# A second layer whose first product is formed from seven block products, with a one-pass softplus

## The chip, the cores and the metric

The kernel runs on one core of a Trainium2 chip. The core has a matrix engine (PE, with its weight loads shown apart as PEld), a vector engine (DVE), an activation engine (ACT), a general engine (POOL), and a queue engine (SP) that issues the transfers here. The metric is the device time of one execution in microseconds, as the median of several runs.

## The reference

Three layers follow one another. All inputs are float32 on the host side apart from the weights, which arrive as 64-bit floats.

```python
x = attention(q, k, v)                  # linear attention, 4 batches x 576 tokens, 8 heads of 64
x = x / rms(x) * rms_g                  # 2304 tokens x 512
x = (silu(x @ w_gate) * (x @ w_val)) @ w_out        # 512 -> 1536 -> 512
h = x @ w2_in                           # 512 -> 2048
g = np.maximum(h, 0) + np.log1p(np.exp(-np.abs(h)))  # softplus
out = g @ w2_out                        # 2048 -> 512
```

## The kernel before

Tokens are cut into NB = 6 blocks of T = 384. Each operand of the two feed-forward layers is split in a high and a low float32r half, and each product is three matrix products (`mm3`, lines 538 to 541: high by high, high by low, low by high). A column tile of a hidden layer is 128 columns wide: 12 tiles in the first layer (FA), 16 in the second (FB). The model dimension of 512 is four row tiles (KD).

The program order of every engine is written out by hand. The string ORDER lists the attention and the first 15 steps of the first layer, mixed. `busy` (B in the list) adds matrix products that compute nothing. From line 775 a loop runs the other 57 of the 72 steps of the first layer (stage A here). A step is one column tile of one token block: `g` (12 matrix products), `v` (12), then the output product `o_step` of the step before (12). After `v`, DVE multiplies (`a`, line 793), ACT rounds to the high half (line 795), and DVE subtracts to get the low half (line 797). Column tiles are taken in groups (GA = 3, 4, 5); the token blocks run inside a group. So one block has 3, 4 or 5 steps in a row. After the last of them the four sums in PSUM are added to `x2t` by DVE (`x2_out`, line 589), and the four input tiles of the next block are split again (`halves`, lines 528 and 536).

The second layer (stage B, from line 857) has 96 steps. One step is `h` for one column tile of one block (12 matrix products of 384 columns), softplus in four ACT and three DVE passes (lines 867 to 882), and the output product `y_step` of two steps earlier (9 matrix products of 512 columns). Sums over a group of column tiles (GB = 6, 5, 5) are added to an SBUF tile by `y_out`. The input tiles of the next block are split by ACT and POOL on the way.

Weights are fetched as 64-bit numbers (`fetch`) and turned into the two halves on the chip: `convert_a` (ACT), `convert_l` and three `convert_d` (DVE), `convert_c` (ACT), `convert_s` (DVE in stage A, POOL in stage B). `at_place(i, p, ...)` puts such a piece at place p of step i, and `do(i, p)` issues it there. Each of the 32 weight tiles of layer two is converted once for the kernel and used by all six blocks of its group.

Of the kernel before, what the change touches and what calls it, by code (L numbers as in the profile page):

```python
# [25 lines left out]
LQ.0.0 LK.0.1.1 Q0.0.0 LX.0 MX.0 LK.0.2.2 QS.0.0.1.P LK.0.0.1 QS.0.0.0.P K0.0.1.1.V QE.0.0.1 QE.0.0.0 K0.0.2.2.V  # L26
LQ.0.1 MV F.7 QR.0.0 B.22 K1.0.2 K0.0.0.1.V LQ.0.2 QI.0.0 KM.0.2 B.2 K1.0.0 CA.7 KM.0.0 F.6 QM.0.0.1.P QM.0.0.0.P
LQ.1.0 K2.0.0 Q0.0.1 KS.0.0 LG Q0.0.2 QS.0.1.1.P LK.1.0.2 QS.0.1.0.P K2.0.2 CL.7.V QE.0.1.0 QS.0.2.0.V T.1 CA.6 KS.0.2
QE.0.2.0 QE.0.1.1 KE.0.0 CL.6.V Q0.1.0 LV.0.0.4 TC.1.A MK LX.1 CD.7.0 QS.1.0.1.P QR.0.1 QI.0.1 QS.1.0.0.P F.3 QE.1.0.1
MX.1 QR.0.2.0 QE.1.0.0 T.0 CA.3 LW.0 LV.0.4.8 QR.1.0 K0.1.0.2.V CD.7.1 KE.0.2 B.28 K3.0.0 CL.3.V CD.7.2 QM.0.1.0.P  # L30
QI.0.2.0 CD.6.0 T.2 QM.0.1.1.P QI.1.0 CD.6.1 K1.1.0 LQ.1.1 TC.0.A QM.1.0.0.P KM.1.0 F.0 TC.2.A QM.0.2.0.P K3.0.2
K4.0.0 K2.1.0 Q0.1.1 LK.1.2.2 K4.0.2 KS.1.0 X0.0.0 X0.0.1 LV.1.0.4 CA.0 SQ.0.1 XG.0.1.A LW.1 XG.0.0.A QS.1.1.1.P
CL.0.V X0.0.2 KE.1.0 K0.1.2.2.V B.4 K1.1.2 X0.0.3 CD.3.0 CD.6.2 XG.0.2.A SQ.0.0 QS.1.1.0.P KM.1.2 F.2 CD.3.1
XS.0.0.1.V K2.1.2 LV.1.4.8 SQ.0.2 QE.1.1.0 QE.1.1.1 SQ.0.3 T.5 XS.0.2.3.P TC.5.A T.3 KS.1.2 F.1 K3.1.0 LX.2 CD.0.0
XS.0.0.2.P CA.2 T.4 QR.1.1 K4.1.0 CL.2.V CD.3.2 CD.0.1 LK.2.0.2 QI.1.1 KE.1.2 CC.7 CA.1 XG.0.3.A TC.4.A QM.1.0.1.P
MX.2 K3.1.2 CL.1.V X1.0 LQ.2.0 TC.3.A B.1 X0.1.1 K4.1.2 CD.1.0 X0.1.3 XG.1.3.A CD.0.2 LK.2.2.2 K0.2.0.2.V X0.1.0
SQ.1.1 XD.0 XG.1.1.A QM.1.1.1.P CD.1.1 Q0.2.0 X0.1.2 SQ.1.2 CC.0 XP.0 LW.2 XG.1.2.A LV.2.0.4 QM.1.1.0.P K1.2.0 CC.3
KM.2.0 SQ.1.3 QS.2.0.0.P T.8 B.1 K2.2.0 T.7 TC.8.A SQ.1.0 TC.7.A T.6 X2.0 K0.2.2.2.V TC.6.A K1.2.2 KS.2.0 KM.2.2
X0.2.0 X0.2.1 XS.1.2.3.V K2.2.2 LV.2.4.8 X3.0.1 F.4 XG.1.0.A CC.6 X3.0.0 X3.0.2 KE.2.0 HH.0.0.A QS.2.0.1.P XS.1.0.1.P
CS.0.P HH.0.2.A HH.0.1.A HL.0.0.P KS.2.2 F.5 HL.0.1.P XS.1.0.2.V K3.2.0 X3.0.3 LQ.2.1 CA.4 LK.3.0.2 G.0.0 LV.3.0.4  # L40
CD.2.0 CL.4.V X1.1 CD.1.2 KE.2.2 HH.0.3.A CC.1 SQ.2.0 LK.3.2.2 CA.5 HL.0.2.V CD.4.0 CD.2.1 HL.0.3.V G.0.1 CS.3.V
CS.1.V K3.2.2 G.0.2 QE.2.0.0 CL.5.V G.0.3 CD.4.1 QE.2.0.1 XD.1 CD.4.2 XP.1 K4.2.2 CD.5.0 MX.3 S.0 V.0 Q0.2.1 CD.5.1
G.1.0 X0.2.2 CC.4 G.1.1 A.0 CS.7.P X2.1 CS.4.P X3.1.2 G.1.2 CS.6.P G.1.3 CD.5.2 S.1 V.1 F.8 X3.1.1 X3.1.0 CC.5 SQ.2.2
QR.2.0 CD.2.2 G.2.0 CS.5.P X3.1.3 G.2.1 QI.2.0 CC.2 G.2.2 HH.1.0.A AH.0.A QM.2.0.1.V XG.2.2.A XG.2.0.A X0.2.3 XG.2.1.A
QS.2.1.0.P G.2.3 A.1 QM.2.0.0.P HL.1.0.V SQ.2.1 T.10 K4.2.0 SQ.2.3 S.2 V.2 LX.3 AL.0.V CS.2.P HH.1.3.A HH.1.1.A G.3.0
F.15 XS.2.0.1.V XG.2.3.A TC.10.A HL.1.3.V HH.1.2.A XS.2.2.3.P XS.2.0.2.V AH.1.A HL.1.1.V CA.8 O.0 HL.1.2.V G.3.1 X1.2
QE.2.1.0 AL.1.P QS.2.1.1.P G.3.2 QE.2.1.1 CL.8.V CA.15 A.2 T.9 TC.9.A CD.8.0 CD.8.1 G.3.3 LQ.3.0 CD.8.2 S.3 AH.2.V
# [27 lines left out]
def linear_attention_swiglu_softplus_kernel(  # L75
# [27 lines left out]
    GA = [3, 4, 5]  # L103
    GB = [6, 5, 5]
    NW = 16
    NX = 6
    BW = P
    YN = 1
    XB = 17
# [4 lines left out]
    assert sum(GA) == FA and sum(GB) == FB and SX * 2 == P and B % 2 == 0  # L114
# [8 lines left out]
    ps_p = ctx.enter_context(tc.tile_pool(name="ps", bufs=1, space=PSUM))  # L123

# [47 lines left out]
    def place(n):  # L172
        return pools[-1] if n in extra else w_p
# [3 lines left out]
    order = [(n, f) for f0, g in groups(GA) for f in range(f0, f0 + g) for n in "gvo"]  # L177
    order += [(n, f) for f0, g in groups(GB) for f in range(f0, f0 + g) for n in "hy"]

    extra = set(range(XB, len(order), 4))  # L180

    def pred(n):
        same = [i for i in range(n) if (i in extra) == (n in extra)]
        size = NX if n in extra else NW
        return same[-size] if len(same) >= size else None
# [52 lines left out]
    def convert_c(n):  # L238
        w = place(n).tile([P, 2, 512], F32R, tag="w", name="w")
        nc.scalar.copy(out=w[:, 0], in_=bits[n].bitcast(F32))  # L240
        wt[order[n]] = w

    def convert_s(n, eng):
        w = wt[order[n]]
        eng.tensor_tensor(out=w[:, 1], in0=bits.pop(n).bitcast(F32), in1=w[:, 0].bitcast(F32), op=ALU.subtract)

# [71 lines left out]
    def k0(b, lo, n, how):  # L318
        hs = slice(2 * lo, 2 * (lo + n))
        km = km_t[:, hs]  # L320
        if how == "R":
            nc.vector.tensor_reduce(out=km, in_=k_t[:, hs].rearrange("p h r d -> p h d r"), op=ALU.max, axis=AX.X)
        else:
            for r in range(1, R + 1):
                nc.vector.tensor_tensor(out=km, in0=km if r > 1 else k_t[:, hs, 0], in1=k_t[:, hs, r], op=ALU.max)  # L325
# [196 lines left out]
    def halves_h(key, src, m, hi="act"):  # L522
        if m == KD - 1 and key[0] == "b":
            t = late[0].tile([P, 2, T], F32R, tag="hl", name="hl")
        else:
            t = hl_p.tile([P, 2, T], F32R, tag="hl", name="hl")
# [22 lines left out]
    with tc.manual_schedule():  # L549
# [73 lines left out]
        def v_step(i):  # L623
# [4 lines left out]
            if not left[j]:  # L628
                for m in range(KD):
                    hl.pop((("a", j), m))  # L630
# [303 lines left out]
```

## Time and profile before

| what | value |
|---|---|
| median of 3 runs | 958.16 us (957.13 to 958.8) |
| the profiled execution | 958.15 us, its span 956.4 us |
| PE busy | 936.2 us (98%) |
| DVE busy | 658.9 us (69%) |
| ACT busy | 504.2 us (53%) |
| POOL busy | 189.0 us (20%) |
| bytes moved by transfers | 55.39 MB |
| mean granted TensorE clock | 0.994 |

The span runs from the first to the last instruction; 1.75 us of the execution lie around it. Busy time of PE is modelled from pipelined products, so the spacing of their starts in the timeline says more than their durations. On the other engines too, two instructions in a row may overlap: the distance of their starts is what one costs when the engine is full.

### The profile page before, as it was taken

The page shows a single profiled execution, that of the slowest core. Times are in us where ns is not written, and L with a number is a line of the kernel's source. Part 1 is how long each engine was busy: PE and PEld are TensorE (multiplying, and loading weights), DVE is VectorE, ACT ScalarE, POOL GpSimd, SP SyncE. Part 2 cuts the span into 40 slices and gives each one's busy share as a digit, 9 for nine tenths or more (in the row PEclk, how much of TensorE's full clock was granted, in tenths as well). Part 3 has the DMA queues.
Part 4 walks back from the last instruction along what each step waited for, and adds up shares of the span by engine and source line. Part 5 has one row for each costly group of instructions (what it writes and reads, how often), then busy time and mean ns, then how long its engine had stood idle before and what let it go on. Part 6 is the DMA issues. An engine that isn't in the chain of part 4 may idle for free.

```text
span 956.4 us, 13447 instructions
## 1 busy us (share of the span) xinstructions
PE 936.2 (98%) x5140; PEld 884.2 (92%) x5140; DVE 658.9 (69%) x1191; ACT 504.2 (53%) x1018; POOL 189.0 (20%) x174
## 2 busy tenths in 40 slices
PE   7789999999999999999999999999999999999998
PEld 7678999999999999999999989999999999999997
DVE  7899988577743377762234677777777888666665
ACT  3567553344422233432122477777777777666664
POOL 4447542400000000000000022222233232212110
PEclk9899999999999999999999999999999999999999
DMA  8992321022200022220000211111111110000111
GB/s 216 220 243 79 97 72 44 24 67 89 89 23 1 1 71 84 88 88 1 1 1 23 66 32 38 42 45 45 45 45 46 45 45 1 1 12 34 45 45 66
DMA packets 64224, 55.39 MB, mean 58 GB/s; under 512 B 25504, under 2 KB 58272, under 8 KB 64160
## 3 DMA queue, kind: packets, MB, share of 16 engines
q1 hardware_dynamic: 64160, 54.54, 19.8%
q8 instruction: 40, 0.66, 0.3%
q14 instruction: 24, 0.20, 0.1%
HBM read 49.81 MB, written 4.72 MB: 57 GB/s over the span
## 4 chain that ended last, share of the span: by engine, by line
PE 87%; DVE 9%; DMA 2%; ACT 1%; issue 1%; SPq 0%; POOL 0%; DVEq 0%; POOLq 0%
PE acc L541 12%; PE acc L540 12%; PE acc L539 11%; PE h L541 7%; PE h L539 7%; PE h L540 7%; PE g L539 5%; PE g L540 5%; PE g L541 5%; PE v L541 5%; PE v L539 5%; PE v L540 5%; PE kvp L376 2%; DVE km_t L325 2%; DVE ke L355 1%
## 5 line engine op out<-in xcount | busy, mean ns | idle before, releaser
L536 POOL TENSOR_TENSOR hl<-x,hl 128x384 fp32r<-128x384 f32 x68 | 70.1, 1032 | 620.0 <-ACT hl L528 535.0
L541 PE MATMUL h<-hl,w 128*128 128x384 f32 x384 | 129.5, 337 | 0.0
L539 PE MATMUL h<-hl,w 128*128 128x384 f32 x384 | 129.3, 337 | 0.0
L540 PE MATMUL h<-hl,w 128*128 128x384 f32 x384 | 128.9, 336 | 0.0
L880 DVE SCALAR_TENSOR_TENSOR u<-u,e 128x384 f32<-128x384 f32 x96 | 55.0, 573 | 82.8 <-ACT ln L877 82.8
L541 PE MATMUL acc<-w,hb 128*128 128x512 f32 x279 | 110.6, 396 | 0.2 <-DVE hb L873 0.2
L540 PE MATMUL acc<-w,hb 128*128 128x512 f32 x279 | 110.2, 395 | 0.0
L539 PE MATMUL acc<-w,hb 128*128 128x512 f32 x279 | 108.5, 389 | 0.0
L539 PE MATMUL g<-hl,w 128*128 128x384 f32 x288 | 101.1, 351 | 0.0
L793 DVE TENSOR_TENSOR a<-s,v 128x384 f32<-128x384 f32 x57 | 31.5, 552 | 97.2 <-PE v L541 97.2
L540 PE MATMUL g<-hl,w 128*128 128x384 f32 x288 | 96.5, 335 | 0.8 <-DVE hl L536 0.8
L539 PE MATMUL v<-hl,w 128*128 128x384 f32 x288 | 97.0, 337 | 0.0
L541 PE MATMUL g<-hl,w 128*128 128x384 f32 x288 | 96.4, 335 | 0.0
L539 PE MATMUL acc<-h,w 128*128 128x384 f32 x288 | 96.3, 335 | 0.0
L540 PE MATMUL acc<-h,w 128*128 128x384 f32 x288 | 96.3, 334 | 0.0
L541 PE MATMUL acc<-h,w 128*128 128x384 f32 x288 | 96.2, 334 | 0.0
L540 PE MATMUL v<-hl,w 128*128 128x384 f32 x288 | 96.2, 334 | 0.0
L541 PE MATMUL v<-hl,w 128*128 128x384 f32 x288 | 96.2, 334 | 0.0
L781 ACT ACTIVATE s<-g 128x384 f32<-128x384 f32 x57 | 28.1, 493 | 127.2 <-PE g L541 127.2
L795 ACT CAST h<-a 128x384 fp32r<-128x384 f32 x57 | 29.3, 514 | 115.6 <-DVE a L793 115.6
L867 ACT ACTIVATE e<-h 128x384 f32<-128x384 f32 x96 | 47.1, 490 | 71.4 <-PE h L541 71.3
L539 PEld LDWEIGHTS h<-hl,w 128*128 128x128 f32 x384 | 72.2, 188 | 4.1
(134 smaller groups left out, 2149.5 us busy)
## 6 DMA issues: line engine op xcount, KB each, us to landing
raw<-in_moe_w_out_dram SPq DMA_DIRECT2D x26, 512.0 KB, 3.5
raw<-in_moe_w_in_dram SPq DMA_DIRECT2D x16, 512.0 KB, 3.7
raw<-in_moe_w_val_dram SPq DMA_DIRECT2D x10, 512.0 KB, 3.6
raw<-in_moe_w_gate_dram SPq DMA_DIRECT2D x10, 512.0 KB, 3.7
qh<-in_q_dram SPq DMA_DIRECT2D x8, 512.0 KB, 5.1
v_t<-in_v_dram SPq DMA_DIRECT2D x32, 128.0 KB, 4.4
out_dram<-y SPq DMA_DIRECT2D x16, 256.0 KB, 2.1
k_t<-in_k_dram SPq DMA_DIRECT2D x7, 512.0 KB, 5.7
```

The lines of the kernel that those rows point to most:

```text
L325: nc.vector.tensor_tensor(out=km, in0=km if r > 1 else k_t[:, hs, 0], in1=k_t[:, hs, r], op=ALU.max)
L355: nc.vector.tensor_tensor(out=ke_t[lo][:, i].rearrange("p r (h d) -> p h r d", d=D), in0=k_t[:, 2 * m:2 * m + 2], in1=bc.to_broadcast([P, ...
L376: nc.tensor.matmul(out=ps[:, i, :], lhsT=ke_t[lo][:p, i, r], rhs=v_t[:p, m, r, :], start=(r == 0), stop=(r == R))
L536: eng.tensor_tensor(out=t[:, 1], in0=src, in1=t[:, 0].bitcast(F32), op=ALU.subtract)
L539: nc.tensor.matmul(out=ps, lhsT=wh, rhs=xh, start=first, stop=False)
L540: nc.tensor.matmul(out=ps, lhsT=wh, rhs=xl, start=False, stop=False)
L541: nc.tensor.matmul(out=ps, lhsT=wl, rhs=xh, start=False, stop=last)
L781: nc.scalar.activation(out=s, in_=g_ps, func=AF.Silu)
L793: nc.vector.tensor_tensor(out=a, in0=s, in1=v_ps, op=ALU.mult)
L795: nc.scalar.copy(out=h[:, 0], in_=a)
L867: nc.scalar.activation(out=e, in_=ps, func=AF.Abs)
L880: nc.vector.scalar_tensor_tensor(out=u, in0=u, scalar=1.0, in1=e, op0=ALU.subtract, op1=ALU.subtract)
```

## The change

- Layer two works on units: two column tiles (f = 2p, 2p+1) by two token blocks (j = 2jp, 2jp+1), with the 512 rows in two halves of 256. The 2 x 2 x 2 block product is formed by seven products (`seven`) of 256 rows instead of eight, Winograd's form: 24 units (NU) of 7 x 6 = 42 matrix products of 384 columns, where 4 steps before had 48. Three sums are kept in the PSUM banks `A` and `B_` and in copies `p1`, `u1`, `p5`. The output product has 36 matrix products per unit, as four steps had; they are put between the seven in twelve parts (`more`).
- Each product needs its own operands. `pair_sums` makes the combinations of the weights, `t_sum` and `split` those of the inputs. GA is [3, 3, 3, 3], and all 32 weight tiles of layer two are converted in stage A (steps 26 to 41 and 51 to 66). Their halves go to DRAM (`keep_h`, `keep_l`), and `load_unit` brings six tiles back for each unit.
- Inputs of the first two blocks are prepared in steps 60 to 70, one piece a step; those of the next two pairs in stage B, in the last two units of the pair before (`ahead`, `ready`).
- Softplus is one ACT pass, with its own table set loaded at the end of stage A. Output sums stay in PSUM over all column tiles of a pair; `y_out` copies them once.
- In the list, `k0` is split into its pieces in the same order, and `busy` counts are 9 larger in sum.

```diff
-    GA = [3, 4, 5]
-    GB = [6, 5, 5]
+    GA = [3, 3, 3, 3]
...
+    def keep_h(dst, src, n=512):
+        w = late[0].tile([P, 2, 512], F32R, tag="ws", name="ws", bufs=NS)
+        nc.scalar.copy(out=w[:, 0, :n], in_=src)
+        return w, dst, src, n
+
+    def keep_l(w, dst, src, n):
+        nc.vector.tensor_tensor(out=w[:, 1, :n], in0=src, in1=w[:, 0, :n].bitcast(F32), op=ALU.subtract)
+        d = kept[dst] = dram.tile([P, 2, n], F32, tag=f"{dst[0]}{dst[1]}", name="kept", bufs=1)
+        nc.sync.dma_start(out=d, in_=w[:, :, :n].bitcast(F32))
+
+    def pair_sums(p, a, b):
+        lo, hi = slice(0, 256), slice(256, 512)
+        t = sums[p] = late[0].tile([P, 3, 256], F32, tag="hb", name="sums", bufs=NH)
+        nc.vector.tensor_tensor(out=t[:, 1], in0=a[:, lo], in1=b[:, lo], op=ALU.subtract)
+        nc.vector.tensor_tensor(out=b[:, lo], in0=b[:, lo], in1=b[:, hi], op=ALU.add)
+        nc.vector.tensor_tensor(out=t[:, 0], in0=b[:, lo], in1=a[:, lo], op=ALU.subtract)
+        nc.vector.tensor_tensor(out=t[:, 2], in0=a[:, hi], in1=t[:, 0], op=ALU.subtract)
...
+        for k, (f, name) in enumerate(prepare):
+            at_place(NA - len(prepare) - 1 + k, 2, f, 0, name)
+        at_place(NA - 4, 3, load_unit, 0)
+        at_place(NA - 1, 3, load_unit, 1)
...
-                nc.scalar.preload_act_table_set("natural_log_exp_and_others")
+                nc.scalar.preload_act_table_set("softplus")
...
+        def activate(u, f, o, src, ln):
+            nc.scalar.activation(out=ln, in_=src, func=AF.Softplus)
...
+            nc.scalar.copy(out=h[:, 0], in_=ln)
+            nc.vector.tensor_tensor(out=h[:, 1], in0=ln, in1=h[:, 0].bitcast(F32), op=ALU.subtract)
...
+        def seven(u, ps, wname, xname, first):
+            jp = u // NPB
+            tile_, o = WHERE[wname]
+            w = wb[tile_, u]
+            x = quad[jp, xname]
+            for m in range(2):
+                c = slice(o * 256 + m * P, o * 256 + (m + 1) * P)
+                mm3(ps, w[:, 0, c], w[:, 1, c], x[m][:, 0], x[m][:, 1], first and m == 0, m == 1, True)
...
+            seven(u, A, "11", "11", True)
+            p1 = fa.tile([P, T], F32, tag="s", name="p1")
+            nc.scalar.copy(out=p1, in_=A)
+            seven(u, B_, "12", "21", True)
+            c11 = late[0].tile([P, T], F32, tag="ln", name="c11")
+            nc.vector.tensor_tensor(out=c11, in0=B_, in1=p1, op=ALU.add)
+            more(1)
+            seven(u, A, "s2", "t2", False)
+            u1 = fa.tile([P, T], F32, tag="a", name="u1")
+            nc.scalar.copy(out=u1, in_=A)
+            activate(u, 0, 0, c11, c11)
+            ready(3)
+            more(1)
+            seven(u, B_, "s1", "t1", True)
+            p5 = fa.tile([P, T], F32, tag="s", name="p5")
+            nc.scalar.copy(out=p5, in_=B_)
+            ready(2)
+            more(1)
+            seven(u, A, "s3", "t3", False)
+            c22 = late[0].tile([P, T], F32, tag="ln", name="c22")
+            nc.vector.tensor_tensor(out=c22, in0=A, in1=p5, op=ALU.add)
+            more(1)
+            seven(u, B_, "s4", "22", False)
+            c12 = fa.tile([P, T], F32, tag="s", name="c12")
+            nc.vector.tensor_tensor(out=c12, in0=B_, in1=u1, op=ALU.add)
+            activate(u, 1, 1, c22, c22)
+            more(1)
+            seven(u, A, "22", "t4", False)
+            c21 = fa.tile([P, T], F32, tag="a", name="c21")
+            activate(u, 1, 0, A, c21)
+            activate(u, 0, 1, c12, c12)
+            ready(3)
+            for f, name in ahead:
+                f(jp + 1, name)
+            more(len(fill))
...
+            load_unit(u + 2)
```

## Rows read from the trace of the kernel before

**Rows 1.** The page: busy time by engine, and the chain that ended last.
```profile
PE 936.2 (98%) x5140; PEld 884.2 (92%) x5140; DVE 658.9 (69%) x1191; ACT 504.2 (53%) x1018; POOL 189.0 (20%) x174
...
PE 87%; DVE 9%; DMA 2%; ACT 1%; issue 1%; SPq 0%; POOL 0%; DVEq 0%; POOLq 0%
```

**Rows 2.** Busy time in stretches (us, instructions), clock, transfer share, GB/s.
```profile
0.00:50.00 50.00, 39.03 (x243) 34.68 (x244) 40.88 (x84) 22.44 (x36) 21.26 (x29) 0.90 0.91 219
...
200.00:250.00 50.00, 50.00 (x291) 50.00 (x290) 39.73 (x75) 21.32 (x43) 0.00 (x0) 1.00 0.28 89
...
350.00:400.00 50.00, 50.00 (x290) 50.00 (x289) 37.14 (x70) 20.10 (x40) 0.00 (x0) 1.00 0.27 85
...
650.00:700.00 50.00, 50.00 (x253) 45.33 (x252) 37.73 (x65) 38.84 (x82) 14.06 (x12) 1.00 0.14 43
```

**Rows 3.** Timeline of PE, last step of stage A: start us, duration, instruction.
```profile
543.39 0.33 PE L539 MATMUL v<-hl,w 128*128 128x384 f32 x1
...
545.47 0.33 PE L539 MATMUL acc<-h,w 128*128 128x384 f32 x1
...
547.55 0.33 PE L539 MATMUL h<-hl,w 128*128 128x384 f32 x1
```

**Rows 4.** Timeline of PE near the end of stage B.
```profile
937.44 0.39 PE L539 MATMUL acc<-w,hb 128*128 128x512 f32 x1
...
939.52 0.33 PE L539 MATMUL h<-hl,w 128*128 128x384 f32 x1
...
952.13 0.39 PE L541 MATMUL acc<-w,hl 128*128 128x512 f32 x1
```

**Rows 5.** Groups by line, whole span: busy, mean ns of one, idle before.
```profile
L870 ACT ACTIVATE e<-e 128x384 f32<-128x384 f32 x96 | 50.2, 523 | 0.1
L852 ACT CAST hb<-ln 128x384 fp32r<-128x384 f32 x93 | 47.5, 511 | 30.6 <-DVE ln L882 29.0
...
L602 PE MATMUL busy<-warm 128*128 128x128 f32 x116 | 16.8, 309 | 1.0 <-DVE nhalf L553 1.0
...
L621 ACT ACT_TABLE_LOAD x4 | 5.1, 1283 | 1.8 <-PE g L541 1.7
```

**Rows 6.** Groups by line on DVE, 198 to 550 us (stage A).
```profile
L797 DVE TENSOR_TENSOR h<-a,h 128x384 fp32r<-128x384 f32 x57 | 31.8, 558 | 33.4 <-ACT h L795 33.4
L793 DVE TENSOR_TENSOR a<-s,v 128x384 f32<-128x384 f32 x57 | 31.5, 552 | 97.2 <-PE v L541 97.2
L536 DVE TENSOR_TENSOR hl<-xn,hl 128x384 fp32r<-128x384 f32 x48 | 23.6, 553 | 22.4 <-ACT hl L528 22.4
L245 DVE TENSOR_TENSOR w<-bits,w 128x512 fp32r<-128x512 f32 x31 | 21.5, 693 | 0.0
L589 DVE TENSOR_TENSOR x<-acc,x 128x384 f32<-128x384 f32 x44 | 21.4, 549 | 0.0
L227 DVE SCALAR_TENSOR_TENSOR bits<-raw,bits 128x512 int32<-128x512 int32 x30 | 20.8, 692 | 1.0
```

**Rows 7.** Timeline of DVE alone, one step of stage A.
```profile
205.25 0.42 DVE L217 TENSOR_SCALAR bits<-bits 128x512 f32<-128x512 f32 x1
...
207.55 1.96 DVE L536 TENSOR_TENSOR hl<-xn,hl 128x384 fp32r<-128x384 f32 x4
209.44 0.55 DVE L793 TENSOR_TENSOR a<-s,v 128x384 f32<-128x384 f32 x1
210.56 0.56 DVE L797 TENSOR_TENSOR h<-a,h 128x384 fp32r<-128x384 f32 x1 [0.58 <-ACT h L795]
211.09 0.69 DVE L245 TENSOR_TENSOR w<-bits,w 128x512 fp32r<-128x512 f32 x1
211.69 0.42 DVE L217 TENSOR_SCALAR bits<-bits 128x512 f32<-128x512 f32 x1
```

**Rows 8.** Groups by line on ACT, 198 to 550 us.
```profile
L528 ACT CAST hl<-xn 128x384 fp32r<-128x384 f32 x48 | 20.9, 512 | 0.0
L212 ACT ACTIVATE bits<-raw 128x512 f32<-128x512 f32 x31 | 20.8, 670 | 0.0
L240 ACT CAST w<-bits 128x512 fp32r<-128x512 f32 x31 | 19.1, 617 | 0.0
```

**Rows 9.** The page: transfer issues, KB each, us from issue to landing.
```profile
raw<-in_moe_w_out_dram SPq DMA_DIRECT2D x26, 512.0 KB, 3.5
```

**Rows 10.** Who waited for whom: us in total, times, longest.
```profile
PE kmT L333 <- DVE km_t L325: 6.6, 4, 2.0
```

More of the change, by code (lines that the diff above doesn't have):

```diff
@@ L31 @@
[L31 to L35, printed above, removed]
@@ L71 @@
+HH.5.3.V HH.5.1.A CS.11.P S.14 X3.5.2 CS.14.V HL.5.3.P AL.13.V V.14 HH.5.0.A A.14 HH.5.2.A AH.14.A HL.5.0.V HL.5.2.V
+O.13 F.16 F.17 AL.14.V HL.5.1.P
 """
@@ L170, in linear_attention_swiglu_softplus_kernel, with ring @@
     pools = [w_p]
-    def place(n):
-        return pools[-1] if n in extra else w_p
+    def ring(n):
+        return w_p if n % RING < NW else pools[-1]
     raws = {}
     bits = {}
[L177 to L185, printed above, removed]
+    first_a = [(n, f) for f in range(FA) for n in "gvo"]
+    pairs_b = [(n, 2 * p + i) for p in range(FB // 2) for n in "hy" for i in range(2)]
+    order = first_a[:27] + pairs_b[:16] + first_a[27:] + pairs_b[16:]
+    number = {t: n for n, t in enumerate(first_a)}
+    RING = NW + NX
     def fetch(n):
@@ L522, in halves_h @@
     def halves_h(key, src, m, hi="act"):
[L523 to L526, printed above, removed]
+        t = hl_p.tile([P, 2, T], F32R, tag="hl", name="hl")
         if hi == "act":
@@ L605, in linear_attention_swiglu_softplus_kernel, with used @@
         left = {}
+        def used(j):
+            left[j] = left.get(j, GA[0] * (KD + 1)) - 1
+            if not left[j]:
+                for m in range(KD):
+                    hl.pop((("a", j), m))
         def g_step(i, m, e=None):
@@ L626, in v_step @@
             kmul(ps[:, :T], wt["v", f], [hl[("a", j), m] for m in range(KD)])
-            left[j] = left.get(j, GA[0]) - 1
-            if not left[j]:
-                for m in range(KD):
-                    hl.pop((("a", j), m))
+            used(j)
         def a_step(i):
@@ L727, in do, with whole, pair_c @@
                 f(*a)
-        lag = 2
-        first_use, last_use = {}, {}
+        def whole(n):
+            return bits[n].bitcast(F32)
+        half = {}
+        def pair_c(n, p, o):
+            name = order[n][0]
+            if (name, o) == ("h", 0):
+                half[0] = keep_h(("x1", p), whole(n))
+            elif (name, o) == ("h", 1):
+                pair_sums(p, whole(n - 1), whole(n))
+                half[1] = keep_h(("x2", p), whole(n))
+            elif o == 0:
+                t = sums[p]
+                half[2] = keep_h(("x3", p), t[:, 0:2].rearrange("p a c -> p (a c)"))
+                half[3] = keep_h(("ya", p), whole(n))
+            else:
+                t = sums[p]
+                half[4] = keep_h(("x4", p), t[:, 2], 256)
+                half[5] = keep_h(("yb", p), whole(n))
@@ new lines, in pair_s @@
+        def pair_s(n, p, o):
+            name = order[n][0]
+            if (name, o) == ("h", 0):
+                keep_l(*half.pop(0))
+            elif (name, o) == ("h", 1):
+                keep_l(*half.pop(1))
+                bits.pop(n - 1)
+                bits.pop(n)
+            elif o == 0:
+                keep_l(*half.pop(2))
+                keep_l(*half.pop(3))
+                bits.pop(n)
+            else:
+                keep_l(*half.pop(4))
+                keep_l(*half.pop(5))
+                bits.pop(n)
+                sums.pop(p)
@@ new lines, in linear_attention_swiglu_softplus_kernel, with load_unit, block @@
+        quad = {}
+        wb = {}
+        tmp = {}
+        count = [0]
+        def load_unit(u):
+            if u >= NU:
+                return
+            for x, name in enumerate(("x1", "x2", "x3", "x4", "ya", "yb")):
+                n = 256 if name == "x4" else 512
+                w = ring(len(first_a) + 6 * u + x).tile([P, 2, 512], F32R, tag="w", name="wb")
+                nc.sync.dma_start(out=w[:, :, :n].bitcast(F32), in_=kept[name, u % NPB])
+                wb[name, u] = w
+        def block(jp, name):
+            r, c = int(name[0]) - 1, int(name[1]) - 1
+            return x2t[2 * jp + c][:, 2 * r:2 * r + 2]
@@ new lines, in split @@
+        def split(jp, name):
+            src = tmp[jp, name] if name[0] == "t" else block(jp, name)
+            k = count[0] % 9
+            count[0] += 1
+            if k < 6:
+                whole = big.tile([P, NCB * DM], F32R, tag=f"xy{k}", name="quad").rearrange("p (m h t) -> p m h t", m=2, h=2)
+                q = [whole[:, m] for m in range(2)]
+                nc.scalar.copy(out=whole[:, :, 0], in_=src)
+                nc.vector.tensor_tensor(out=whole[:, :, 1], in0=src, in1=whole[:, :, 0].bitcast(F32), op=ALU.subtract)
+            else:
+                q = [hl_p.tile([P, 2, T], F32R, tag="hl", name="quad") for m in range(2)]
+                for m in range(2):
+                    nc.scalar.copy(out=q[m][:, 0], in_=src[:, m])
+                    nc.vector.tensor_tensor(out=q[m][:, 1], in0=src[:, m], in1=q[m][:, 0].bitcast(F32), op=ALU.subtract)
+            quad[jp, name] = q
@@ new lines, in linear_attention_swiglu_softplus_kernel, with y_out @@
+        out_n = [0]
+        def y_out(jp, o, t):
+            ps = acc.pop((jp, o, t))
+            y = late[0].tile([P, 2, 512], F32, tag="ws", name="y", bufs=NS)[:, 0]
+            out_n[0] += 1
+            if out_n[0] % 2:
+                nc.vector.tensor_copy(out=y, in_=ps)
+            else:
+                nc.scalar.copy(out=y, in_=ps)
+            pair, ci = divmod((2 * jp + o) * NCB + t, CPP)
+            if ci == R:
+                for d in range(2):
+                    r0 = (2 * pair + d) * S + SM
+                    nc.sync.dma_start(out=out[r0:r0 + SX, :], in_=y[d * SX:(d + 1) * SX])
+            else:
+                b, r = (2 * pair, ci) if ci < R else (2 * pair + 1, ci - R - 1)
+                nc.sync.dma_start(out=out[b * S:b * S + SM, :].rearrange("(p r) e -> p r e", r=R)[:, r, :], in_=y)
@@ L902, in linear_attention_swiglu_softplus_kernel, with o_parts, part @@
-        y_out(NCB)
+                    y_out(jp, o, t)
+            return [
+                (part, (o, f, t, p == 0 and k == 0, p == NPB - 1 and k == 1))
+                for o, fs in ((0, (0, 1)), (1, (1, 0)))
+                for k, f in enumerate(fs)
+                for t in range(NCB)
+            ]
+        def o_parts(i):
+            h = act.pop(("a", i))
+            w = wt["o", stepsA[i][2]]
+            def part(m):
+                c = slice(m * P, (m + 1) * P)
+                mm3(acc[m][:, :T], w[:, 0, c], w[:, 1, c], h[:, 0], h[:, 1], False, True)
+                x2_out(i, m, "V")
+            return [(part, (m,)) for m in range(KD)]
```

312 lines of the change are left out of this document (139 added, 173 removed).

## The prediction

> **What bounds the kernel now.** I read the page first: PE is busy for 98% of the span and makes 87% of the chain that ended last [rows 1]. Then the stretches: from 200 us on PE fills every 50 us, while DVE is at 37 to 40 us of 50 where weights are converted [rows 2]. Then the timeline, for the distance of starts. In stage A 12 products of 384 columns take 545.47 - 543.39 = 2.08 us, 0.1733 each, and the next 12 the same [rows 3]; a step of 36 takes 6.24 us. In stage B nine products of 512 columns take 939.52 - 937.44 = 2.08 us, 0.231 each [rows 4]. So PE runs without gaps from 200 us to its last product, and two things count: how many products go away, and how long PE must now wait for others.
>
> **What is saved on PE.** 24 units by 6 products of 384 columns are 144 products; the output products keep their number. At 0.1733 that is 25.0 us. A second way: stage B runs from 547.55 to about 952.13 + 0.23 [rows 3, 4], 404.8 us; less 2.08 for the last output product of layer one and 864 x 0.231 = 199.7, it leaves 203.0 us for 1152 products, 0.1762 each, so 25.4 us. I take 25.2.
>
> **What costs nothing while its cover lasts.**
> - Softplus: three of four ACT passes of about 0.52 us [rows 5] and three DVE passes per tile go; they hid behind PE. If the new pass cost two of the old, a unit would have 3 copies, 4 passes and 4 roundings: 3 x 0.5 + 4 x 1.05 + 4 x 0.51 = 7.7 us of ACT in 15.6 us of PE (7 x 1.04 + 36 x 0.231). The set change was there before. Roundings beside Silu and Exp caused no set change of their own: the four loads of line 621 belong to the changes between those two [rows 5].
> - In an ordinary unit each PSUM bank is read while PE works elsewhere. The tightest place is `A`: the first product ends at 1.04 us, the copy `p1` takes 0.5, and PE comes back to `A` at 2.77 after another product and one output part (0.69). Later places have over a microsecond too.
> - Loads in stage B: five tiles of 512 KB and one of 256 KB, 2.88 MB per unit of 15.6 us, are 185 GB/s. At the start 219 GB/s passed at a share of 0.91, and 89 GB/s took 0.28 [rows 2], so about 240 to 320 GB/s are there, and a tile is asked for over a unit ahead. SP's queue holds only these loads and the output stores. If this cover were gone, the second rival tells the price.
> - The stores of converted halves in stage A, at most 1.0 MB beside a fetch of 0.5 MB in a step of 6.24 us, are 250 GB/s in one step of four and 195 on average. A fetch has nine microseconds until it is needed, and SP's next entry waits behind a store only for a subtraction that DVE does in the same step.
> - Nine more `busy` calls at 2 x 0.145 us (16.8 / 116 [rows 5]) are 2.6 us at most, and PE waited 6.6 us before the products that follow them [rows 10]: nothing, at worst 2.6.
> - The tail is as before: one copy, then one store.
>
> **What DVE must now do in stage A.** Distances of starts [rows 7]: converting one tile takes 207.55 - 205.25 = 2.30 us up to the next work; four `halves` 1.89 (0.47 each); from `a` to the end of the low half 211.09 - 209.44 = 1.65, with 0.58 idle inside; a subtraction of 512 columns 0.60. By the slope between 384 and 512 columns, 256 cost 0.34 and 768 cost 0.88 (durations would be 0.41 and 0.97 [rows 6]). Three steps of one block that convert tiles of layer one need 3 x (2.30 + 1.65 + 0.60) + 1.89 + 4 x 0.47 for `x2_out` = 17.4 us, against 18.7 us of PE. So the smaller groups alone cost nothing, though they add 24 `x2_out` and 24 `halves`. In a step that converts a tile of layer two, `keep_l` and `pair_sums` add: first h tile 0.60; second h tile four sums of 256 columns (1.55 with their dependences, less the idle 0.58) and 0.60, so about 1.55; first y tile 1.20; second 0.95. The mean is 1.07. A block needs 3 x (2.30 + 1.65 + 1.07) + 1.89 + 1.88 = 18.8 us against 18.7. DVE is just full. It may lag: the first product of the next block waits once DVE enters a block's third step over 3.6 us late (6.41 less 2.30 less 0.47), and the output product waits for its banks once `x2_out` ends over 5.6 us into the next step. Going step by step through 26 to 41, the lag at a step's start rises from 1 to at most 3.25 us, and not at a third step: no wait of PE. From 51 to 59 it is the same. From 60 to 66 each step also gets a sum or a split of 768 columns, 0.9 us. The lag at the start of steps 60 to 67 becomes 1.8, 3.8, 3.6, 5.3, 6.4, 5.7, 5.5 and 6.9 us, and PE waits 0.85 in step 64, 2.0 after step 65, and 1.35 in step 67: **4.2 us**. After that no conversions are left and DVE catches up. The bounds: nothing, if each instruction is a few per cent cheaper; 15 us, if each costs its full duration. I take 4.2, as the distances were measured in the same stage.
>
> **What preparing inputs does in stage B.** In the last unit of the first and of the second pair, five pieces stand between the copies that PE waits for. On ACT two roundings of 768 columns (0.83 each, by the slope of [rows 8]) stand ahead of `p5`. They wait for the sum t2, which on DVE follows the low half of c11 (to 5.95 us of the unit) and ends at 6.9. So `p5` ends near 8.9, and the sixth product, due at 7.97, starts 1.0 late. Then DVE has two splits, t3 and a third split, whose rounding waits for t3, ahead of `c22`: it ends near 12.8, and the last product, due at 10.7, waits 2.1. With a little for each handover 3.3 us per unit, **6.6 us** for two; bounds 0 (all early) and 13. In the first unit only four output parts of 0.52 us stand between the products, so the softplus that reads `A` ends after PE is back at `A`: **0.7 us**.
>
> **Sum.** Against the profiled execution, 958.15 us, which stands at the median of the runs (958.16): 958.15 - 25.2 + 4.2 + 6.6 + 0.7 = **944.5 us**.
>
> **The rivals.**
> - *Little waiting.* DVE keeps up and the preparation hides: 958.15 - 25.2 + 0 to 5 = 933 to 938 us. For it: DVE is over its limit by only 0.1 us a block outside steps 60 to 66, and lags are absorbed. Against it: `c22` stands behind three splits in DVE's own order.
> - *DVE takes the whole duration of each instruction.* Then a block needs 3 x (2.23 + 1.69 + 1.25) + 8 x 0.55 = 19.9 us, 1.2 over PE. 32 steps give 12.6, seven pieces 6.6, and about 2.2 are absorbed in each half: 15 us in place of 4.2, so 955 us. Against it: four subtractions of 0.553 [rows 6] lie within 1.96 us, and their follower starts 1.89 after the first [rows 7]. The Trainium skill speaks for it (VectorE: DVE Perf Modes, The DRAIN you can't avoid): the next instruction does not start until the pipe of the one before is empty. By that rule the sum would be 955; this trace disagrees, with 0.47 between starts of 0.553 each.
> - *Slower: the loads of stage B come one after the other.* A 512 KB fetch takes 3.5 us from issue to landing [rows 9]. Five of these and half of one are 19 us per unit against 15.6, so 24 x 3.6 = 86 us more: 1030 us. It decides from a rate of 2.88 MB / 16.1 us = 179 GB/s downwards, where the unit loses what the seven products and the waits leave. Against it: 219 GB/s at the start, with many transfers in flight [rows 2]. The Trainium skill (DMA: Bandwidth & Descriptors, Bandwidth) asks for 1 MiB or more in a transfer for three quarters of the peak; these are half of that. No run here shows that peak, and the trace shows only that the rate of the first 50 us is enough.
> - *The seven products don't run at the spacing of before*, because PE changes more often between 384 and 512 columns. The two ways of counting above differ by 0.003 us a product, which bounds this at 3 us here: 947 us. It lies in the forecast's spread.
>
> **How the numbers follow.** Forecast with its spread (939 to 950): 0.60. Little waiting (933 to 939): 0.15. DVE at full duration, or both waits twice as long (950 to 957): 0.15. Slower by the loads, or by a wait in each unit that I don't see: 0.10. The range from 935 to 955 leaves out the slow case, the edge of the third and the lowest two microseconds, about 2 in 10. A measurement of this kernel can tell about 0.2%, 1.9 us, from no change: faster than 956.2 us 0.85, within 0.2% 0.06, slower 0.09.
>
> **What the profile of the changed kernel would show.** The groups of `seven` hold 1008 products of 384 columns with starts 0.173 us apart. PE fills each 50 us from 200 to about 490 us. DVE is near full in the stretches of steps 26 to 41 (about 260 to 360 us) and 51 to 66 (415 to 520 us), and PE waits for DVE only near 500 us, at the low half of an input or at `x2_out`. In stage B PE waits for `p5` and `c22` in two places, about 125 us apart, and else hardly. The transfer share in stage B is 0.55 to 0.75 at 185 GB/s. The prediction is wrong if PE waits in every unit, if PE waits for a weight tile, if DVE holds PE up already before step 60, or if the spacing of products grows.

## The result, and the profile after

The changed kernel takes 945.94 us (945.33 to 945.96, 4 runs), the kernel before 958.48 us in the same set of runs. The ratio is 0.9862, with a 95% interval from 0.9847 to 0.9877. Forecast were 944.5 us and a range from 935 to 955. The profiled execution took 945.95 us, its span is 944.2 us, 12.2 us shorter than the one of before.

In the page of the changed kernel, the first line is busy time by engine (share of the span, instructions), the second the chain that ended last.

```profile
PE 917.5 (97%) x5014; PEld 864.1 (92%) x5014; DVE 583.8 (62%) x1100; ACT 403.2 (43%) x788; POOL 87.6 (9%) x85
...
PE 82%; DVE 12%; issue 2%; DMA 2%; ACT 1%; POOL 0%; SPq 0%; DVEq 0%; POOLq 0%; ACTq 0%
```

DVE has 75 us less to do than in [rows 1], ACT and POOL 101 us each, yet DVE's share of the chain rose from 9 to 12%: PE is still the bound, with a few waits for DVE. The stretches of the changed kernel, with the columns of [rows 2] (busy us and instructions of PE, PEld, DVE, ACT, POOL; clock; transfer share; GB/s), show where:

```profile
300.00:350.00 50.00, 50.00 (x290) 50.00 (x289) 45.48 (x90) 24.11 (x49) 0.00 (x0) 1.00 0.58 203
350.00:400.00 50.00, 50.00 (x291) 50.00 (x290) 43.34 (x84) 22.45 (x46) 0.00 (x0) 1.00 0.40 132
...
500.00:550.00 50.00, 47.06 (x269) 46.16 (x268) 36.37 (x67) 20.20 (x40) 0.00 (x0) 1.00 0.60 218
...
600.00:650.00 50.00, 50.00 (x250) 45.14 (x249) 12.28 (x23) 17.04 (x35) 0.00 (x0) 1.00 0.52 174
650.00:700.00 50.00, 47.18 (x226) 41.76 (x225) 22.83 (x36) 22.89 (x45) 0.00 (x0) 0.97 0.37 125
700.00:750.00 50.00, 50.00 (x250) 45.19 (x249) 12.26 (x23) 17.13 (x35) 0.00 (x0) 1.00 0.71 254
750.00:800.00 50.00, 47.80 (x236) 42.44 (x234) 18.26 (x32) 19.08 (x39) 0.00 (x0) 1.00 0.52 174
```

PE is full through the first conversions of layer-two tiles (to 360 us), although DVE is at 45.5 of 50 us there. It lacks more than a microsecond only in 500 to 550, 650 to 700 and 750 to 800 us, and in stage B DVE is busy for a quarter of the time in between. PE's waits for other engines that bear on this, in total, with the number of times and the longest one:

```profile
PE hA L562 <- DVE c L1041: 3.7, 2, 2.1
PE g L563 <- DVE hl L559: 2.7, 3, 1.7
PE hB L562 <- ACT p L1036: 1.7, 2, 0.9
PE acc L562 <- DVE x L608: 1.3, 2, 0.9
PE hA L562 <- ACT c L921: 0.6, 1, 0.6
```

These are `c22` (line 1041), the low halves of a next block (559; one of the three, 0.8 us, stands before 200 us), `p5` (1036), `x2_out` (608) and the softplus that reads `A` (921). The "idle" of a wait is counted from the modelled end of the product before. What PE lost is the distance of two starts less the normal one (0.1733 or 0.231 us), about 0.17 us more per wait. The start after that comes about 0.1 us late as well. Losses by distances of starts, below, hold both.

### The profile page after: what moved, and what is told of

Read it like the earlier page. It is cut to its first block, busy times and chain, and to the rows that moved or that the text cites. A ratio compares the mean times of both kernels' runs of the same rounds, so it can differ in the third digit from the quotient of the medians.

```text
span 944.2 us, 13203 instructions
## 1 busy us (share of the span) xinstructions
PE 917.5 (97%) x5014; PEld 864.1 (92%) x5014; DVE 583.8 (62%) x1100; ACT 403.2 (43%) x788; POOL 87.6 (9%) x85
## 4 chain that ended last, share of the span: by engine, by line
PE 82%; DVE 12%; issue 2%; DMA 2%; ACT 1%; POOL 0%; SPq 0%; DVEq 0%; POOLq 0%; ACTq 0%
PE acc L563 11%; PE acc L564 11%; PE acc L562 11%; PE g L563 4%; PE g L562 4%; PE v L563 4%; PE v L564 4%; PE v L562 4%; PE g L564 4%; PE hA L562 4%; PE hA L564 4%; PE hA L563 4%; PE hB L564 3%; PE hB L563 3%; PE hB L562 2%; PE kvp L402 2%
## 5 line engine op out<-in xcount | busy, mean ns | idle before, releaser
L928 DVE TENSOR_TENSOR hb<-c,hb 128x384 fp32r<-128x384 f32 x69 | 38.4, 556 | 81.9 <-ACT hb L927 81.9
L564 PE MATMUL acc<-wb,hb 128*128 128x512 f32 x207 | 81.5, 394 | 0.0
L563 PE MATMUL acc<-wb,hb 128*128 128x512 f32 x207 | 81.5, 394 | 0.0
L562 PE MATMUL acc<-wb,hb 128*128 128x512 f32 x207 | 80.7, 390 | 0.0
L562 PE MATMUL hA<-quad,wb 128*128 128x384 f32 x192 | 65.0, 339 | 4.3 <-DVE c L1041 3.7
L1026 DVE TENSOR_TENSOR c<-hB,p 128x384 f32<-128x384 f32 x24 | 13.4, 558 | 84.4 <-PE hB L564 81.4
L564 PE MATMUL hA<-quad,wb 128*128 128x384 f32 x192 | 65.5, 341 | 0.0
L563 PE MATMUL hA<-quad,wb 128*128 128x384 f32 x192 | 65.5, 341 | 0.0
L563 PEld LDWEIGHTS g<-hl,w 128*128 128x128 f32 x288 | 54.2, 188 | 5.0 <-DVE hl L559 3.8
L921 ACT ACTIVATE c<-c 128x384 f32<-128x384 f32 x72 | 37.7, 524 | 45.2 <-DVE c L1041 45.2
L562 PEld LDWEIGHTS acc<-h,w 128*128 128x128 f32 x288 | 54.1, 188 | 2.0 <-issue 1.9
L562 PEld LDWEIGHTS g<-hl,w 128*128 128x128 f32 x288 | 54.2, 188 | 1.5
```

The costliest lines, as they stand in the source:

```text
L562: nc.tensor.matmul(out=ps, lhsT=wh, rhs=xh, start=first, stop=False, skip_group_check=more)
L563: nc.tensor.matmul(out=ps, lhsT=wh, rhs=xl, start=False, stop=False, skip_group_check=more)
L564: nc.tensor.matmul(out=ps, lhsT=wl, rhs=xh, start=False, stop=last, skip_group_check=more)
L921: nc.scalar.activation(out=ln, in_=src, func=AF.Softplus)
L928: nc.vector.tensor_tensor(out=h[:, 1], in0=ln, in1=h[:, 0].bitcast(F32), op=ALU.subtract)
L1026: nc.vector.tensor_tensor(out=c11, in0=B_, in1=p1, op=ALU.add)
```

## The experiments

All runs were compared with the kernel before on the same chip; it came out at 958.5 to 960.2 us there, so close times are set side by side by ratio. Differences of ratios are turned into time with 958.5 us.

**1. The preparing pieces of stage A in steps 67 to 71.**

```diff
-            at_place(NA - len(prepare) - 1 + k, 2, f, 0, name)
+            at_place(NA - 5 + (0, 0, 1, 1, 2, 2, 2, 3, 3, 4, 4)[k], 2, f, 0, name)
```

> The eleven pieces that prepare the inputs of the first two blocks (sums and splits of 768 columns) stand in steps 67 to 71, two or three a step, where no weight is converted any more, and not in steps 60 to 70. Theory (DVE is just full with the conversions, and the pieces on top make PE wait): the four waits of PE near 492, 503, 512 and 524 us go, which is 4.2 us: 941.7 us. Rival (DVE takes the whole duration of its instructions, so the conversions alone hold PE up): most of the waits stay, 944 to 946 us. Rival (preparation comes too late for the first unit): a wait at the start of the second layer takes the place, 945 us or more.

Measured: 941.6 us, ratio 0.9815 [0.98, 0.983], 4.5 us less than the changed kernel. All waits of PE in the second half of stage A are gone. The four were, in the changed kernel and by distances of starts: 0.48 us after step 62, 0.62 in step 64, 1.94 after step 65, 1.15 in step 67, together 4.2 us. The largest two stand so in the timeline of PE in the changed kernel:

```profile
512.02 0.34 PE L562 MATMUL g<-hl,w 128*128 128x384 f32 x1
514.02 0.45 PE L563 MATMUL g<-hl,w 128*128 128x384 f32 x1 [1.66 <-DVE hl L559]
...
524.22 0.34 PE L564 MATMUL v<-hl,w 128*128 128x384 f32 x1
525.46 0.41 PE L562 MATMUL acc<-h,w 128*128 128x384 f32 x1 [0.90 <-DVE x L608]
```

And DVE around the first of them, in the same kernel:

```profile
508.88 0.43 DVE L265 TENSOR_TENSOR sums<-bits,sums 128x256 f32<-128x256 f32 x1
509.22 0.55 DVE L909 TENSOR_TENSOR h<-a,h 128x384 fp32r<-128x384 f32 x1
509.69 0.69 DVE L254 TENSOR_TENSOR ws<-bits,ws 128x512 fp32r<-128x512 f32 x1
510.29 0.95 DVE L867 TENSOR_TENSOR quad<-t,quad 128x768 fp32r<-128x768 f32 x1
511.16 0.42 DVE L217 TENSOR_SCALAR bits<-bits 128x512 f32<-128x512 f32 x1
511.62 0.43 DVE L223 TENSOR_SCALAR bits<-bits 128x512 int32<-128x512 int32 x1
512.08 0.69 DVE L227 SCALAR_TENSOR_TENSOR bits<-raw,bits 128x512 int32<-128x512 int32 x1
512.81 0.69 DVE L231 SCALAR_TENSOR_TENSOR bits<-raw,bits 128x512 int32<-128x512 int32 x1
513.41 1.96 DVE L559 TENSOR_TENSOR hl<-xn,hl 128x384 fp32r<-128x384 f32 x4
```

DVE has no gap at all, and starts on the halves of the next block (513.41) when PE already stands at its second product (512.19 would have been its time). The split of 768 columns holds DVE from 510.29 to 511.16, 0.87 us, where the prediction used 0.88.

**2. One more subtraction in each of the 32 steps that convert a tile of layer two.**

```diff
+            w, _, s2, m = half[{("h", 0): 0, ("h", 1): 1, ("y", 0): 3, ("y", 1): 5}[name, o]]
+            nc.vector.tensor_tensor(out=w[:, 1, :m], in0=s2, in1=w[:, 0, :m].bitcast(F32), op=ALU.subtract)
             if (name, o) == ("h", 0):
```

> Each of the 32 steps that convert a weight tile of the second layer makes one of its subtractions twice: 32 x 0.60 us more on DVE, 19.2 us in all. Theory (DVE is just full in these steps, one instruction costs the distance of starts): lags can no longer be worked off, PE waits in blocks from the third on: 945.9 + 16 = 962 us (955 to 966). Rival (there is room on DVE in these steps outside 60 to 66): under 5 us more, 946 to 951 us.

Measured: 967.77 us, ratio 1.0078 [1.0061, 1.0095], 20.7 us more than the changed kernel, just outside the expected 955 to 966. PE now loses time where the changed kernel had none:

```profile
300.00:350.00 50.00, 44.19 (x249) 42.65 (x248) 44.56 (x88) 20.92 (x44) 0.00 (x0) 1.00 0.50 179
350.00:400.00 50.00, 47.85 (x275) 47.24 (x274) 44.27 (x87) 20.35 (x42) 0.00 (x0) 1.00 0.42 142
```

PE's waits in stage A grow from 3.8 to 23.3 us. The edit gives DVE more than the 19.2 us of the expectation. In the 16 steps that convert h tiles it writes one tile twice in a row, and these two starts are 0.72 us apart, not 0.60. In the 16 steps of y tiles the extra subtraction stands ahead of one that is ready, and DVE waits for ACT's rounding, which it never did here in the changed kernel:

```profile
DVE ws L777 <- ACT ws L250: 6.0, 16, 0.5
```

That makes 16 x 0.72 + 16 x 0.60 + 6.0 = 27 us more on DVE, of which 19.5 come out as waits of PE. So DVE has about 0.2 us to spare in each of these steps, less than one instruction, and a lag can hardly be worked off before the next one. The expectation was short by 4 us. Beside the waits, 1.3 us are the late products behind them, and 3.1 us were lost at half clock, behind the two largest waits (2.55 and 2.51 us, near 509 and 533 us; granted clock 0.93 in 500 to 550 us). Stage B is 1.5 us shorter than in the profile of the changed kernel, which has a stretch at half clock there.

**3. The preparing pieces of stage B behind p5 and c22.**

```diff
             activate(u, 0, 0, c11, c11)
-            ready(3)
...
             nc.scalar.copy(out=p5, in_=B_)
-            ready(2)
...
             nc.vector.tensor_tensor(out=c22, in0=A, in1=p5, op=ALU.add)
+            ready(2)
...
             activate(u, 1, 1, c22, c22)
+            ready(2)
...
             activate(u, 0, 1, c12, c12)
-            ready(3)
+            ready(4)
```

> In the last unit of the first and of the second pair of blocks, no preparing piece stands ahead of the copy p5 or of the sum c22 any more: two stand behind c22, two behind the softplus of c22, four at the end. Theory (PE waited for p5 and c22 only because of the pieces ahead of them): the waits of 1.0 and 2.3 us in the one unit and 1.2 and 1.9 us in the other go, and the stretch at half clock behind the first of them too (1.2 us): 938 to 940 us. Rival (ACT and DVE have too little room in such a unit, wherever the pieces stand): waits of the same size appear at the next unit's p1 or c11, 945 us. Which of the two: where PE waits between 650 and 690 us.

Measured: 937.49 us, ratio 0.977 [0.9756, 0.9785], 8.8 us less than the changed kernel and just under the expected 938 to 940. By distances of starts 3.4 and 3.2 us of waits went, and a stretch at half clock that cost 1.55 us, not 1.2. PE has no wait between 564 us and its last product. In the changed kernel the timeline of PE in the last unit of the first pair reads:

```profile
664.85 0.40 PE L564 MATMUL acc<-wb,h 128*128 128x512 f32 x1
666.00 0.44 PE L562 MATMUL hB<-quad,wb 128*128 128x384 f32 x1 [0.76 <-ACT p L1036]
...
667.62 0.40 PE L564 MATMUL acc<-wb,h 128*128 128x512 f32 x1
670.08 0.45 PE L562 MATMUL hA<-quad,wb 128*128 128x384 f32 x1 [2.06 <-DVE c L1041]
```

The timeline of DVE alone in the same unit:

```profile
663.03 0.95 DVE L856 TENSOR_TENSOR t<-x,t 128x768 f32<-128x768 f32 x1
664.88 1.83 DVE L867 TENSOR_TENSOR quad<-t,quad 128x768 fp32r<-128x768 f32 x2 [0.90 <-ACT quad L866]
666.74 0.96 DVE L856 TENSOR_TENSOR t<-x 128x768 f32<-128x768 f32 x1
668.60 0.96 DVE L867 TENSOR_TENSOR quad<-t,quad 128x768 fp32r<-128x768 f32 x1 [0.90 <-ACT quad L866]
669.47 0.55 DVE L1041 TENSOR_TENSOR c<-hA,p 128x384 f32<-128x384 f32 x1
```

And that of ACT alone:

```profile
664.01 1.57 ACT L866 CAST quad<-t 128x768 fp32r<-128x768 f32 x2 [1.49 <-DVE t L856]
665.48 0.47 ACT L1036 COPY p<-hB 128x384 f32<-128x384 f32 x1
667.73 0.83 ACT L866 CAST quad<-t 128x768 fp32r<-128x768 f32 x1 [1.78 <-DVE t L856]
```

It is the chain of the prediction: two splits and their sum ahead of `p5`, then t3 and a third split ahead of `c22`, each engine waiting for the other by turns. Moved behind, the same work costs nothing.

**4. Both orders.** The edits of 1 and 3 together.

> Both changes of order together. Theory (the two groups of waits have nothing to do with each other): 945.9 - 4.2 - 7.5 = 934.2 us, and PE waits from 200 us to the end for under 1.5 us. Rival (one hides the other): above 937 us.

Measured: 934.0 us, ratio 0.9732 [0.9713, 0.9751], 12.5 us less than the changed kernel and the fastest version here. From 200 us to the end of its last product PE waits for one thing, the softplus that reads `A` in the first unit:

```profile
PE hA L562 <- ACT c L921: 0.6, 1, 0.6
```

The two gains add up (4.5 and 8.8 against 12.5 us).

**5. Eight block products again.**

```diff
             seven(u, A, "11", "11", True)
+            seven(u, A, "11", "11", True)
```

> Each unit makes its first product twice (the second starts the sum anew), so it has eight block products again with everything else as in the changed kernel: 144 matrix products of 384 columns more. Theory (the gain is the number of products at 0.1733 us each): 945.9 + 25.0 = 971 us, less up to 0.9 where PE waits anyway at the start of the second unit. Rival (the gain comes partly from fewer passes on ACT and DVE and from POOL doing nothing): clearly less than 25 us more, for instance 955 to 965 us.

Measured: 969.53 us, ratio 1.0103 [1.0087, 1.0118], 23.1 us more by ratio. From the first to the last start of a product in stage B it is 410.8 us, against 387.4 in the changed kernel: 23.4 more. The waits are those of the changed kernel, but this profile has no stretch at half clock behind the first preparing unit, which there costs 1.55 us (see below). 23.4 + 1.55 = 25.0 us, the same as 144 products at 0.1733. The gain is the number of products.

**6. Softplus in four ACT passes and three DVE passes.**

```diff
+            d = h[:, 1]
+            for _ in range(3):
+                nc.scalar.activation(out=d, in_=src, func=AF.Softplus)
             nc.scalar.activation(out=ln, in_=src, func=AF.Softplus)
+            for _ in range(3):
+                nc.vector.tensor_tensor(out=d, in0=ln, in1=ln, op=ALU.subtract)
```

> Softplus is made in four ACT passes of the same size, and three DVE passes stand ahead of the subtraction, as many as before the change; the extra ones are overwritten. Theory (softplus in one pass gives nothing by itself, PE hides it): ordinary units stay at 15.6 us; only the second unit's start and the two units that prepare wait longer, by 1 to 3 us each: 948 to 953 us. Rival (the one-pass softplus carries a part of the gain, since a unit needs its chain of copies in time): over 0.5 us in each of 24 units, 958 us or more.

Measured: 970.44 us, ratio 1.0103 [1.0083, 1.0124]: 23.1 us more than the changed kernel, and slower than the kernel before. The theory has the ordinary units right and the price wrong; the rival has a price that fits (958 us or more), but not for its reason, a loss in every unit. This is an ordinary unit:

```profile
590.00:606.00 16.00, 16.00 (x82) 14.46 (x81) 10.54 (x20) 11.16 (x23) 0.00 (x0) 1.00 0.55 183
```

PE is full with ACT at 11.2 of 16 us. The whole price lies in few places. By distances of starts PE loses 5 us in the first two units and 9 and 12 us in and behind the two units that prepare (longest waits 3.9 and 4.1 us, for `p5`), where the changed kernel loses 0.9, 3.4 and 3.2, and 7 us at half clock, against 1.55. The extra ACT passes stand ahead of the one that counts, and those of `c21` read bank `A`, which they hold for longer: the largest wait of the first two units, 3.4 us, is for it. So this is the price of the passes in this placement.

**7. The same passes with both orders changed.** The edits of 4 and 6 together.

> Four ACT passes and three DVE passes for softplus as in the experiment before, now with both orders of preparation changed. With the order of the changed kernel the extra passes cost 24 us, all of it in waits at the first units of the layer and in and behind the two units that prepare. Theory (in ordinary units PE hides the passes; the cost came from preparing pieces that stood ahead of PE's next copies on a fuller ACT): 934 us and about 5 at the first two units and up to 3 for each preparing unit, 938 to 946 us. Rival (the passes are too many for a preparing unit in any order, or cost something in each unit): 952 us or more.

Measured: 963.53 us, ratio 1.005 [1.0035, 1.0065], 30.5 us more than experiment 4 by ratio, so the rival's number holds. PE loses 5.2 us in the first two units and about 9 us at each preparing one; stretches at half clock follow the long waits. The longest wait stands behind the first of those, and in its stretch DVE is the full engine:

```profile
676.00:686.00 10.00, 3.56 (x18) 2.66 (x16) 9.59 (x15) 6.83 (x13) 0.00 (x0) 0.82 0.00 0
```

PE has 3.56 of 10 us, DVE 9.59. PE waits for `p1`, which stands on ACT behind the last rounding, and that waits 2.95 us for the sum t4 on DVE. By an estimate from these rows, DVE has 10.5 us to do in an ordinary unit (the window of experiment 6) and 8 x 0.87 us more for the pieces, 17.5 us, where PE has 15.7. That no other order would do, over more units for instance, is not shown; none was tried beyond these two. With the one-pass softplus it has room: in experiment 4 DVE is at 24 of 50 us in 650 to 700 us.

**8. Twice the transfers in stage B.**

```diff
                 nc.sync.dma_start(out=w[:, :, :n].bitcast(F32), in_=kept[name, u % NPB])
+                spare_d = dram.tile([P, 2, n], F32, tag=f"z{name}{u % NPB}", name="spare", bufs=1)
+                nc.sync.dma_start(out=spare_d, in_=kept[name, u % NPB])
```

> Beside each tile that a unit loads, the same bytes are also copied from DRAM to another place in DRAM: twice the traffic, 5.8 MB per unit of 15.6 us, 370 GB/s. Theory (the transfers run side by side, with about 330 to 350 GB/s to be had by the shares of the changed kernel, so that a single load stream at 185 GB/s is far from its limit): the unit becomes 16.5 to 17.5 us long and PE waits for weight tiles: 945.9 + 20 to 45 us. Rival (the load stream of the changed kernel is already near its limit): a unit of over 25 us, over 1150 us.

Measured: 944.4 us, ratio 0.9839 [0.9822, 0.9857]: no longer than the changed kernel. Both expectations missed. The transfers ran, and PE never waited for a tile:

```profile
700.00:750.00 50.00, 50.00 (x251) 45.16 (x250) 12.28 (x23) 17.14 (x35) 0.00 (x0) 1.00 1.02 419
```

419 GB/s passed, more than the 370 that the units ask for, and more than the 330 to 350 read from shares of the changed kernel (188 GB/s at a share of 0.57, for instance, would be 330 at 1).

**9. Three times the transfers.** Two such copies beside each load.

> Two copies from DRAM to DRAM beside each tile that a unit loads: three times the traffic, 8.65 MB per unit, 554 GB/s at 15.6 us. With twice the traffic 419 GB/s passed and PE never waited for a tile. Theory (419 GB/s is what there is, and only then the loads bound a unit): 20.6 us per unit, 5.0 more in some 20 to 23 units, 1040 to 1065 us, and PE waits for weight tiles. Rival (tiles are asked for so early, or copies yield to loads, that PE hardly waits): under 960 us.

Measured: 1102.09 us, ratio 1.1494 [1.1463, 1.1525], above the expected 1040 to 1065. Now PE waits for tiles, 19 times at a product into `A`, and twice for `p1` (the waits of PE, and one of the stretches):

```profile
PE hA L562 <- DMA wb<-kept: 74.8, 19, 5.2
PE hA L562 <- ACT p L1026: 41.0, 2, 20.7
...
600.00:650.00 50.00, 37.65 (x166) 33.17 (x164) 8.18 (x15) 11.23 (x23) 0.00 (x0) 0.90 1.02 387
```

The loads bound the units, as expected, but 387 GB/s pass, not 419, so 8.65 MB take 22.4 us per unit and not 20.6. That alone is 6.8 us more in some 22 units, 150 us, which gives 1095 against 1102. The units do not share it evenly. In the second unit of the second and of the third pair, which take 39 us each, ACT and DVE stand still for 23.6 us before an output copy: its buffer is free only when an earlier output has been stored, and that store stands in SP's queue behind the loads and copies. `p1` stands behind that copy, and PE waits over 20 us for it. The expectation did not have this wait. Transfers go on meanwhile (busy share 0.89 and 0.85), and the unit that follows each takes 15.7 us.

**10. The changed kernel once more**, beside experiments 7 and 9.

> The changed kernel itself once more, beside the next two on the same chip: 945 to 948 us, as the kernel before came out 1 to 1.7 us longer beside the other experiments than beside the first measurement.

Measured: 944.85 us, ratio 0.9855 [0.9835, 0.9875], the same as the first time (0.9862).

## Why the prediction was right

- *Products.* 144 fewer at 0.1733 us. Experiment 5 puts the price of the same number at 25.0 us. With both orders changed (experiment 4) stage B takes 379.4 us from its first start of a product to its last, against 404.6 in the kernel before: 25.2 us, with 0.85 us of waits left in it and 0.95 in the kernel before. The step holds. Those 0.95 us, near 556, 565 and 948 us, the prediction's "without gaps" passes over.
- *DVE in stage A.* 4.2 us forecast, 4.2 measured. The waits forecast for steps 64, 65 and 67 were 0.85, 2.0 and 1.35; they were 0.62, 1.94 and 1.15, and one of 0.48 stood after step 62, for which the working gave just none. Experiment 1 shows the preparing pieces as their cause, experiment 2 that DVE has hardly any room without them. The slope gives 0.86 us for 768 columns, not the 0.88 of the working; 0.87 was measured.
- *Preparing in stage B.* 6.6 us forecast; by distances of starts 3.38 in the one unit (1.04 + 2.34) and 3.17 in the other (1.22 + 1.95), 6.55 in all. Experiment 3 shows the order as the cause. Not in the sum were 1.55 us at half clock behind the first.
- *First unit.* 0.7 forecast, 0.85 measured.
- *The sum.* From its first start to its last, stage B is 17.2 us shorter, with 8.95 us of losses in it, so 26.2 went: the products and the 0.95 us of before. 26.2 less 4.2, 6.55, 1.55 and 0.85, and less 0.8 by which the first 200 us are longer, is 12.2 us, the difference of the spans. So the terms of the forecast hold to 0.2 us, and what it left out cancels in part: 1.0 us more went, against 1.55 at half clock and 0.8 in the first 200 us. That near half of what was left out cancelled is luck. The 0.8 can't be told from chance: in the profiles of the changed kernel and of the experiments the same step of stage A starts between 235.2 and 238.4 us, at 235.6 in the kernel before. What the nine `busy` calls cost is therefore not shown.
- *Rivals.* DVE at full duration per instruction: rejected. The 768 columns last 0.95 us and hold DVE for 0.87 (experiment 1's lines), the sum would have been 955, and in experiment 1 no wait of stage A is left. The Trainium skill's rule of the emptied pipe (VectorE: DVE Perf Modes, The DRAIN you can't avoid) does not fit this trace. The same paragraph of it says that a next instruction which is not held back starts earlier, and with that the 0.87 agrees; the prediction does not have this half. Loads one after the other: rejected by experiment 8, where 419 GB/s pass, and the limit shows in experiment 9. Little waiting: both groups of waits were there; experiment 4 shows that they could be avoided, at 934.0 us. Another spacing of products: rejected. In stage B the starts come to 2.6 us more than the same counts at 0.1733 and 0.231 in the kernel before, and to 2.3 in the changed one, without the losses.
- *What the prediction had wrong* without harm to its number: "Softplus ... they hid behind PE" was taken from ordinary units and used for all. In ordinary units it holds (experiment 6). But seven block products with as many passes as before, placed as in experiment 6, come out slower than the kernel before, 970 against 960 us, because the units that prepare, and the first two, have no room for them. The term of zero was right for the change as it stands, and wrong as a statement on what the one-pass softplus is worth: it carries 23 us in this placement. The estimate of the transfer rate, 240 to 320 GB/s, was too low, and so most stretches of stage B are at a transfer share of 0.52 to 0.57, where 0.55 to 0.75 was forecast.

## What to carry to other kernels

When a saving on the bounding engine is paid for with work on a quiet one, add up that engine's work per block with distances of starts, not durations, and follow its lag step by step: it may be full for long without harm, and of one more instruction per step most of the length then comes out as a wait (19.5 of 27 us in experiment 2). Place optional work behind the copies that the bounding engine waits for, and look at the few units that do extra work: they, not the ordinary ones, decide whether a second part of a change is free. A rate worked out from a busy share can be well below what transfers reach (330 to 350 against 419 GB/s here).

## What the runs showed that was not expected

After the two gaps in the first preparing unit (0.9 and 2.2 us lost, 1.8 us of products between them) the granted clock fell to half. These are the windows of the changed kernel:

```profile
667.00:670.00 3.00, 1.01 (x5) 0.54 (x3) 2.10 (x4) 0.83 (x1) 0.00 (x0) 1.00 0.28 115
670.00:672.00 2.00, 1.92 (x7) 1.91 (x8) 1.04 (x3) 1.15 (x3) 0.00 (x0) 0.68 0.00 0
672.00:674.30 2.30, 2.30 (x7) 1.77 (x6) 0.93 (x2) 2.23 (x5) 0.00 (x0) 0.54 0.00 0
674.30:677.00 2.70, 2.70 (x14) 2.23 (x13) 2.67 (x4) 1.16 (x2) 0.00 (x0) 1.00 0.00 0
```

From 670.7 to 674.2 us products of 384 columns started 0.32 us apart, in place of 0.17, and those of 512 columns 0.43, in place of 0.23: the level of 1.2 GHz, not 2.4. In all it cost 1.55 us. It happened in the profiles of the changed kernel (both of them) and of experiments 1 and 8. It did not happen in those of experiments 2 and 5, with gaps of the same length in the same unit, nor in any of these at the second preparing unit (1.1 and 1.9 us). Two gaps close together are not needed: in experiment 2 the same spacing of 0.32 us appears behind the single waits of 2.55 and 2.51 us in stage A, for over 3 us each. Why it comes in one profile and not in another stays open.
